# Lightning attention followed by a four-expert MoE: values and scores in one run, scores in two banks of the second product

## The chip, the cores and the metric

The kernel runs on one core of one Trainium2 chip. The metric is the device time of one execution in microseconds; the median of the runs counts. Everything is fp32.

## The reference

Two stages. The first is a linear attention with a decay per head, over 4 batches, 8 heads, 768 positions and 64 channels a head, in blocks of 64 positions with a running state:

```python
for b in range(nb):                                   # 12 blocks of 64
    intra = einsum('bhic,bhjc->bhij', qb, kb) * Dmask
    intra = einsum('bhij,bhjd->bhid', intra, vb)
    inter = einsum('bhid,bhde->bhie', qb * lam_pow, kv_state)
    out[:, :, sl] = intra + inter
    kv_state = lam_block * kv_state + einsum('bhsd,bhse->bhde', kb * rev_pow, vb)
```

Its output, laid out as x (3072 tokens by 512), goes through four experts that are all applied to every token:

```python
p = domain_probs / (domain_probs.sum(-1, keepdims=True) + 1e-09)
for e in range(4):                                    # w1[e] 512x1024, w2[e] 1024x512
    out += p[:, e:e+1] * (maximum(x @ w1[e], 0) @ w2[e])
```

## The kernel before

The tokens are cut into 24 chunks of 128 and three groups of eight chunks. A unit is one group through one expert; there are twelve units, 0 to 11, group by group. Both matrix products of a unit are computed in the manner of Strassen, as seven products of half-size blocks (M1 to M7). The products of the second layer of one unit (`second_product`, the matmuls at L1134, used in units 0 to 4) are interleaved with the products of the first layer of the next unit (`first_product`, L1075), which are themselves split into seven smaller products. All engines' orders are written out by hand: the program emits instructions in the order of the main loop, with a running slot count `now[0]`, and each engine executes its own in that order.

**Slots.** A unit has seven products, a product eight slots, so that slot s is (unit x 7 + product) x 8 + x. Slots take turns: a fourth of the second product (eight matmuls of 128x128 by 128x256 as the trace counts them), then a part of the first product (eight, in one slot of eight four). At the end of a slot come the vector and scalar work that was put off (`lately`, `background`, one item taken per slot), then the steps of the attention that are due in it, then loads and stores.

**The attention.** Chunks 0 to 7 (group 0) are computed in a prologue. Chunks 8 to 23 are computed in the main loop, in units 0 to 3, at slots that a formula gives: chunk n belongs to s = 24 + 12 x (n - 8).

- `load_more(n)` at s - 10 loads q and k (SP's queue, L174, or L114 for the chunks that come across); `load(n, "v")` at s - 6 loads v (L114).
- `turn(n)` at s brings q and k into the layout that scores need: eight PE transposes (L670) into PSUM banks s0 and s1, copied out by ScalarE, and q scaled from PSUM by VectorE. Chunks 16 to 23 come across: they are loaded from a DRAM buffer already in part turned, and two VectorE transposes of a whole tile (L652) take the place of those of PE.
- `scores(n)` at s + 5, or s + 6 for those that come across: 16 matmuls of q and k (L700) and 16 of v and k for the states (L707), all 64x64 (the trace records each twice), into banks s0 and s1. VectorE masks them into tile st and adds the states.
- `values(n)` at s + 10, or s + 12: 16 matmuls of the scaled q with the state (L754) and 16 of v with the masked scores (L772), again into s0 and s1. ScalarE copies the result out (L793).

Work on the chunk's tiles is put off by `soon` into `lately`, and taken at later slots, one item at a time; values forces what is still open. The decay of k is done on POOL. The state of a batch is one tile of two halves (for the two blocks of a chunk), of which POOL carries the first into the second.

**Banks.** PSUM has eight banks: s0, s1 for the attention, g1 and g3 for the first product, q01, q02, q11, q12 for the second. Of the second product's seven steps, in the order M1, M7, M4, M6, M2, M5, M3, the banks q02 and q12 are used by M7, M4 (steps 1, 2) and M2 (step 4); M1, M6, M5, M3 use q01 and q11. VectorE adds a bank's content to the results (L1152).

**Tiles.** q, k, v, the states, the masked scores and the sums of the first product all come out of one pool of 42 tiles of 128x512 (`small`), whose tags are shared: a load waits until the last reader of the tile that it replaces is done. All loads and stores of this stretch are issued by SP, in order (`send`, L114).

**The x blocks.** The output of the attention for group 1 goes to DRAM as seven blocks (`pair_sums`, `x_blocks`) and is fetched again by `x_fill`, which issues two loads (tile xs) and for some blocks differences on POOL, at slot 3 of each of seven successive products. `FILL` gives the product of the first. The first layer of group 1 starts at product 21, beside the last unit of group 0.

`forget`, called at the start of unit 4, takes all that is still open in `lately`.

Of the kernel before, what the change touches and what calls it, by code (L numbers as in the profile page):

```python
# [12 lines left out]
ALU = mybir.AluOpType  # L13
# [8 lines left out]
def kernel(  # L22
# [30 lines left out]
    nc = tc.nc  # L53
# [9 lines left out]
    CPG = 8  # L63
# [28 lines left out]
    def small(name):  # L92
        return pool.tile([P, W], FP32, name=name, tag="t")
# [22 lines left out]
    def tt(eng, o, a, b, op):  # L116
        eng.tensor_tensor(out=o, in0=a, in1=b, op=op)  # L117
        if eng is nc.gpsimd:
            busy[0] = max(busy[0], now[0]) + math.prod(o.shape[1:]) / (640 if spare else 480)
        else:  # L120
            vector(math.prod(o.shape[1:]), PSUM in (a.space, b.space))

    def vector(n, psum):
        filled[0] = max(filled[0], now[0] + psum / 2) + 0.09 + n * (0.31 if psum else 0.8 if spare else 0.49) / 512
# [29 lines left out]
    def after_of(n):  # L154
        c, b = where(n)
        return next((m for m in range(n + 1, NG * CPG) if where(m) == (c + 1, b)), None)
# [41 lines left out]
    def all_added(still=None):  # L198
        while adds and (still is None or adds[0][0] < still):
            adds.pop(0)[1]()  # L200
# [342 lines left out]
    def scale_q(qs, of):  # L543
        by = q_decay.unsqueeze(2).to_broadcast([P, NHP, 2, BL])
        tt(nc.vector, by_block(qs), by_block(of), by, ALU.mult)

    def passed(eng, o, s):
        tt(eng, o, s, q_decay[:, :, BL - 1:BL].to_broadcast([P, NHP, D]), ALU.mult)
# [68 lines left out]
    def soon(n, *work):  # L617

        if n < CPG:
            background[0:0] = work  # L620
            rest(len(work))
        else:
            lately.extend(work)
# [8 lines left out]

    carried = set()

    def begin_state(n):
        if where(n)[0] == 0 and n not in states:
            states[n] = small("kv")[:].rearrange("p (x h d) -> p x h d", x=2, d=D)
        if where(n)[0] and n in states and n not in carried:
            carried.add(n)
            passed(nc.gpsimd, states[n][:, 1], states[n][:, 0])  # L640

    def turn_across(n):

        qT, kT = nat.pop((n, "qx")), nat.pop((n, "kx"))
        qs = small("qs")

        def scaled():
            scale_q(qs, qT)
            turned[n] = qT, kT, qs

        def across(x):
            nc.vector.transpose(out=x[:], in_=x[:])  # L652
            vector(W, False)

        soon(n, *(lambda x=x: across(x) for x in (qT, kT)), scaled)

    def turn(n, tags):
        all_added()
        begin_state(n)
        if comes_across(n):  # L660
            turn_across(n)
            return
        if n < CPG:
            decayed(n)
        qn, kn = nat.pop((n, "q")), nat[n, "k"]
        qp = bank(tags[0], "qp")
        kp = bank(tags[1], "kp")
        for x, y in ((qp, qn), (kp, kn)):
            for ac in range(NHP):
                nc.tensor.transpose(  # L670
                    out=x[:, ac * C:(ac + 1) * C], in_=y[:, 2 * ac:2 * ac + 2].rearrange("p r d -> p (r d)"),
                    identity=ident[:],
                )
        if n >= CPG:
            decayed(n)
        del nat[n, "k"]
        qT, kT, qs = small("qT"), small("kT"), small("qs")
        nc.scalar.copy(out=qT[:], in_=qp[:])
        nc.scalar.copy(out=kT[:], in_=kp[:])
        scaled = lambda: scale_q(qs, qp)  # L680
        soon(n, scaled)
        turned[n] = qT, kT, qs, scaled

    def scores(n, tags):
        all_added()
        while n not in turned:
            take(lately, True)
        qT, kT = turned[n][0:2]
        while any(f in lately for f in turned[n][3:]):
            take(lately, True)  # L690
        begin_state(n)
        kd, vn = nat.pop((n, "kd")), nat[n, "v"]
        first, last = where(n)[0] == 0, where(n)[0] == NCH - 1

        sp = [bank(tags[r], "sp") for r in range(2)]
        blk = [slice(x * BL, (x + 1) * BL) for x in range(2)]
        for ac in range(NHP):
            for r in range(2):
                for x in range(2):
                    nc.tensor.matmul(  # L700
                        out=sp[r][half[x], ac * BL:(ac + 1) * BL], lhsT=hc(kT)[half[r], ac, blk[x]],
                        rhs=hc(qT)[half[r], ac, blk[x]], start=(ac == 0), stop=True, skip_group_check=True,
                    )
        for ac in range(NHP):
            for x in range(1 if last else 2):
                for r in range(2):
                    nc.tensor.matmul(  # L707
                        out=sp[x][half[r], 256 + ac * D:256 + (ac + 1) * D], lhsT=kd[half[x], 2 * ac + r],
                        rhs=vn[half[x], 4 * r + ac], start=False, stop=True, skip_group_check=True,
                    )  # L710
        st = small("st")
        added = [sp[x][:, 256:512].rearrange("p (h d) -> p h d", d=D) for x in range(2)]

        def mask(r):
            tt(
                nc.vector, st[:, r * 256:(r + 1) * 256], sp[r][:, 0:256], s_decay[:, r].rearrange("p h c -> p (h c)"),
                ALU.mult,
            )

        def middle():  # L720
            s = states[n][:, 1]
            if first:
                nc.scalar.copy(out=s, in_=added[0])
            else:
                tt(nc.vector, s, s, added[0], ALU.add)

        def end():
            s = states[after_of(n)] = small("kv")[:].rearrange("p (x h d) -> p x h d", x=2, d=D)
            passed(nc.vector, s[:, 0], states[n][:, 1])
            tt(nc.vector, s[:, 0], s[:, 0], added[1], ALU.add)  # L730

        work = [lambda: (mask(0), mask(1)), middle] + ([] if last else [end])
        soon(n, *work)
        masked[n] = st, work

    def values(n, tags):
# [15 lines left out]
        def inter(a, r, x, start):  # L752
            for y in range(2):
                nc.tensor.matmul(  # L754
                    out=op[r][half[y], cols(a, r) if x == r else apart(a)], lhsT=state[half[r], x, 2 * a + y],
                    rhs=by_block(qs)[half[r], 2 * a + y, x], start=start, stop=False, skip_group_check=True,
                )

# [55 lines left out]
            made.add(("blocks", g, x)),  # L814
        ))

    FILL = {1: 18, 2: 43}
    BEGIN = {1: (24, 12), 2: (24 + 12 * CPG, 12)}
    steps = []

    def attention(g):

        def put(slot, f):
            steps.append((slot, f))

        for i in range(CPG):
            n, s = g * CPG + i, BEGIN[g][0] + BEGIN[g][1] * i
            put(s - 10, lambda n=n: load_more(n))
            put(s - 6, lambda n=n: load(n, "v"))
            put(s, lambda n=n: turn(n, ("s0", "s1")))  # L830
            if comes_across(n):
                put(s - 2, lambda n=n: (decayed(n), nat.pop((n, "k"))))
            put(s + (6 if comes_across(n) else 5), lambda n=n: scores(n, ("s0", "s1")))
            put(s + (12 if comes_across(n) else 10), lambda n=n: values(n, ("s0", "s1")))
            if n == NG * CPG - 1:
                put(s + 17, turn_gates)
        steps.sort(key=lambda s: s[0])

    def forget():
        while lately:  # L840
            take(lately, True)
        assert not states


    rows = {
# [838 lines left out]
        "M2": ((), (), (("M3", 0, 0), ("M3", 0, 1)), (), (("M3", 1, 0), ("M3", 1, 1))),  # L1684
        "M4": ((("M5", 0),), (("M5", 1),), (("M2", 0),), (("M2", 1),)),
    }
    for g in range(1, NG):
        attention(g)
    PACE = 1.0, 1.0, 1.0
    FEED = (1, 5), (2, 5)  # L1690
    first_steps = first_result()
    for at, (g, e) in enumerate(units):
# [9 lines left out]
            chores.extend(prepare_w2_ops(1, True))  # L1702
            spare.append(True)
        if at == NEST - 1:
            forget()
            packed.append(True)
        blocks, banks = {}, {}
        for i in range(7):
# [40 lines left out]
            for x, part in enumerate(order):  # L1749
# [6 lines left out]
                if joins:  # L1756
                    joined()
                elif (ahead or x % 2 == 0 and x + i) and not (nests and i == 6 and x == 7):
                    if nested or nests:
                        rest()  # L1760
                    else:
                        took = False
                        for of in (lately, background, own_sums):
                            if of and (not took or fits() or of is background and len(of) > 1):
                                take(of)
                                took = True
# [22 lines left out]
                        x_fill(h, SEQ[at * 7 + i - FILL[h]])  # L1789
                pump(PACE[g])  # L1790
    pump(force=True)
    assert not (first_steps or ending or background or aside or chores or queue or late or results)


# [26 lines left out]
```

## Time and profile before

| what | value |
|---|---|
| median of three runs | 1157.88 us (1155.69 to 1158.87) |
| span of the profiled execution | 1157.0 us |
| PE (matmul) busy | 1143.7 us, 99% |
| PEld (weight load) busy | 991.6 us, 86% |
| VectorE (DVE) busy | 788.8 us, 68% |
| POOL busy | 771.7 us, 67% |
| ScalarE (ACT) busy | 369.8 us, 32% |
| HBM read, written | 194.83 MB, 77.10 MB |

The span is the time from the first to the last recorded instruction of one execution. Busy shares are averages; where an engine is on the path that sets the end is seen in its waits and in the chain that ended last. In that chain TensorE has 89% of the span, and the two products of the main loop that matter here have most of it: L1075 37% and L1134 20%. The costliest groups there (busy us in total, mean ns of one, then the idle time before them and what ended it):

```profile
L1075 PE MATMUL pg<-xs,ws_in 128*128 128x256 f32 x1960 | 472.9, 381 | 3.1 <-DVE m L117 2.9
L1134 PE MATMUL q<-w2t,m 128*128 128x256 f32 x1120 | 265.7, 380 | 0.5 <-DVE m L117 0.5
```

Matmuls are pipelined: each is on record for 380 ns, but the next starts before it ends. So the price of work on TensorE is read from the starts.

### The profile page before, as it was taken

The page shows a single profiled execution, that of the slowest core. Times are in us where ns is not written, and L with a number is a line of the kernel's source. Part 1 is how long each engine was busy: PE and PEld are TensorE (multiplying, and loading weights), DVE is VectorE, ACT ScalarE, POOL GpSimd, SP SyncE. Part 2 cuts the span into 40 slices and gives each one's busy share as a digit, 9 for nine tenths or more (in the row PEclk, how much of TensorE's full clock was granted, in tenths as well). Part 3 has the DMA queues.
Part 4 walks back from the last instruction along what each step waited for, and adds up shares of the span by engine and source line. Part 5 has one row for each costly group of instructions (what it writes and reads, how often), then busy time and mean ns, then how long its engine had stood idle before and what let it go on. Part 6 is the DMA issues. An engine that isn't in the chain of part 4 may idle for free.

```text
span 1157.0 us, 22155 instructions
## 1 busy us (share of the span) xinstructions
PE 1143.7 (99%) x8011; PEld 991.6 (86%) x8011; DVE 788.8 (68%) x1428; ACT 369.8 (32%) x745; POOL 771.7 (67%) x731
## 2 busy tenths in 40 slices
PE   8999999999999999999999999999999999999998
PEld 7888888888888888888888888888888888888887
DVE  3676775478477757835775567989775566676785
ACT  3422123222312321222244442343354442342332
POOL 2738318547742974873784998895995783873884
PEclk8999999999999999999999999999999999999999
DMA  8796668999899999896957667976777757657542
GB/s 189 181 276 190 185 178 243 291 295 282 264 319 311 267 304 303 264 352 180 293 189 243 185 203 252 344 225 202 220 244 247 214 175 196 196 160 215 167 191 74
DMA packets 309260, 269.22 MB, mean 233 GB/s; under 512 B 141536, under 2 KB 244128, under 8 KB 309152
## 3 DMA queue, kind: packets, MB, share of 16 engines
q1 hardware_dynamic: 290832, 262.53, 74.0%
q10 hardware_dynamic: 18320, 5.28, 2.3%
q8 instruction: 64, 1.05, 0.4%
q14 instruction: 44, 0.36, 0.1%
HBM read 194.83 MB, written 77.10 MB: 235 GB/s over the span
## 4 chain that ended last, share of the span: by engine, by line
PE 89%; DVE 5%; POOL 3%; issue 1%; DMA 1%; ACT 1%; ACTq 0%; SPq 0%; DVEq 0%; POOLq 0%
PE pg L1075 37%; PE pq L1433 20%; PE q L1134 20%; PE pM L1535 3%; DVE m L117 2%; PE pc L1535 2%; POOL acc L117 1%; PE sp L700 1%; DVE sums L117 1%; PE op L754 1%; PE op L772 1%; PE sp L707 1%; POOL ops L117 1%; DVE xs L117 1%; PE qp L670 1%
## 5 line engine op out<-in xcount | busy, mean ns | idle before, releaser
L1075 PE MATMUL pg<-xs,ws_in 128*128 128x256 f32 x1960 | 472.9, 381 | 3.1 <-DVE m L117 2.9
L1075 PEld LDWEIGHTS pg<-xs,ws_in 128*128 128x128 f32 x1960 | 368.7, 190 | 59.1 <-DVE m L117 8.9
L117 DVE TENSOR_TENSOR m<-pg,m 128x512 f32<-128x512 f32 x374 | 255.1, 686 | 102.0 <-PE pg L1075 90.4
L1134 PE MATMUL q<-w2t,m 128*128 128x256 f32 x1120 | 265.7, 380 | 0.5 <-DVE m L117 0.5
L1134 PEld LDWEIGHTS q<-w2t,m 128*128 128x128 f32 x1120 | 211.9, 190 | 30.1 <-DVE m L117 1.1
L117 POOL TENSOR_TENSOR m<-m,decay 128x512 f32<-128x512 f32 x91 | 115.6, 1284 | 89.4 <-ACT m L1092 62.8
L117 DVE TENSOR_TENSOR sums<-pq,sums 128x256 f32<-128x256 f32 x272 | 112.7, 420 | 85.7 <-PE pq L1433 77.7
L1433 PE MATMUL pq<-acc,w2t 128*128 128x256 f32 x688 | 169.2, 379 | 0.0
L1433 PEld LDWEIGHTS pq<-acc,w2t 128*128 128x128 f32 x688 | 130.5, 190 | 18.0
L1092 ACT ACTIVATE m<-m 128x512 f32<-128x512 f32 x99 | 62.4, 630 | 191.9 <-DVE m L117 189.9
L117 DVE TENSOR_TENSOR m<-m,m 128x512 f32<-128x512 f32 x112 | 100.4, 896 | 5.9 <-ACT m L1058 5.9
L1152 DVE SCALAR_TENSOR_TENSOR acc<-q,gate,acc 128x256 f32<-128x256 f32 x108 | 51.9, 480 | 75.3 <-PE q L1134 75.0
L1088 ACT COPY m<-pg 128x512 f32<-128x512 f32 x88 | 51.6, 586 | 123.8 <-PE pg L1075 122.4
L1052 ACT COPY pg<-m 128x512 f32<-128x512 f32 x77 | 45.4, 590 | 133.4 <-DVE m L117 126.2
L117 POOL TENSOR_TENSOR acc<-hT,hT 128x512 f32<-128x512 f32 x56 | 71.3, 1289 | 18.2 <-PE pq L1433 15.7
L117 POOL TENSOR_TENSOR acc<-hT,acc 128x512 f32<-128x512 f32 x56 | 71.4, 1275 | 8.5 <-PE pq L1433 4.7
L1433 PE MATMUL pq<-hT,w2t 128*128 128x256 f32 x288 | 70.0, 379 | 0.0
L117 POOL TENSOR_TENSOR w2o<-w2b 128x512 f32<-128x512 f32 x26 | 36.1, 1411 | 48.0 <-DMA w2b<-in_moe_w_dram 31.5
L1433 PEld LDWEIGHTS pq<-hT,w2t 128*128 128x128 f32 x288 | 54.5, 190 | 7.7
L1433 PE MATMUL pq<-m,w2t 128*128 128x256 f32 x228 | 55.5, 379 | 0.0
L117 POOL TENSOR_TENSOR xs<-xs 128x256 f32<-128x256 f32 x28 | 24.7, 884 | 43.3 <-DMA xs<-x_blocks 41.7
L907 ACT COPY hp<-m 128x512 f32<-128x512 f32 x84 | 48.4, 589 | 16.0 <-DVE hT L117 15.0
(145 smaller groups left out, 1443.2 us busy)
## 6 DMA issues: line engine op xcount, KB each, us to landing
w2t<-w_ops SPq DMA_DIRECT2D x129, 256.0 KB, 3.2
ws_in<-w_ops SPq DMA_DIRECT2D x40, 512.0 KB, 4.5
ws_in<-w_ops SPq DMA_DIRECT2D x60, 256.0 KB, 4.0
ws_in<-w_ops SPq DMA_DIRECT2D x40, 384.0 KB, 4.2
w2b<-in_moe_w_dram SPq DMA_DIRECT2D x56, 256.0 KB, 5.4
w_ops<-ops SPq DMA_DIRECT2D x28, 512.0 KB, 4.6
w2t<-w_sums SPq DMA_DIRECT2D x40, 256.0 KB, 4.6
w_sums<-w2o SPq DMA_DIRECT2D x16, 512.0 KB, 5.1
```

What stands on the lines that cost most here:

```text
L117: eng.tensor_tensor(out=o, in0=a, in1=b, op=op)
L670: nc.tensor.transpose(out=x[:, ac * C:(ac + 1) * C], in_=y[:, 2 * ac:2 * ac + 2].rearrange("p r d -> p (r d)"), identity=ident[:],)
L700: nc.tensor.matmul(out=sp[r][half[x], ac * BL:(ac + 1) * BL], lhsT=hc(kT)[half[r], ac, blk[x]], rhs=hc(qT)[half[r], ac, blk[x]], start=(ac ...
L907: nc.scalar.copy(out=there[x][:], in_=blk[at][:])
L1052: nc.scalar.copy(out=banks[tags[1]][:], in_=new["11"][:])
L1075: nc.tensor.matmul(out=p[:, j * 256:(j + 1) * 256], lhsT=ws[i][:, j * P:(j + 1) * P], rhs=xs[i], start=(fresh and j == 0), stop=True, skip ...
L1088: nc.scalar.copy(out=new[at][:], in_=p[:])
L1092: nc.scalar.activation(out=new[at][:], in_=new[at][:], func=AF.Relu)
L1134: nc.tensor.matmul(out=p[:, s * DH:(s + 1) * DH], lhsT=h[A_OF[m]][:, c * 256 + s * P:c * 256 + (s + 1) * P], rhs=fed2[g, e, m][uu][:, c], ...
L1152: nc.vector.scalar_tensor_tensor(out=o, in0=x, scalar=w, in1=o, op0=ALU.mult, op1=ALU.add)
L1433: nc.tensor.matmul(out=p[:, 0:256], lhsT=fed3[e, m, x // 2][:, x % 2, c * P:(c + 1) * P], rhs=b[B_OF[i]][:, c * 256:(c + 1) * 256], start= ...
L1535: nc.tensor.matmul(out=p[:, s * 256:(s + 1) * 256], lhsT=a[c][:, f:f + P], rhs=b[:, c, j * 256:(j + 1) * 256], start=(s == 0 and c == 0 an ...
```

## The change

In the main loop, chunks 8 to 23 are placed by a list of slots `AT` instead of a formula. At the slot of chunk n, the values of chunk n - 1 (in s0 and s1) and the scores of chunk n (now in q02 and q12) are emitted one right after the other. Around it:

- The turn stands 3 slots ahead of it, or 5 for chunks that come across; q and k are loaded 5 or 4 slots ahead of the turn, v 3 slots ahead of the scores. The k decay of chunks that come across is put 2 slots ahead of their turn.
- q is no longer scaled into a tile of its own out of PSUM: the copy of q is scaled in place after the scores, as the last item of the chunk's put-off work.
- The halves of a state are given out one by one out of a tile, and a new state takes a half.
- The x blocks of group 1 are fetched from product 20 on, not 18.
- `turn_gates` (the gates of the last group) stands 14 slots ahead of the last scores. `all_added` is told the current slot by `scores`; `forget` is gone; in unit 4, an open item of `lately` is taken ahead of `background`.

```diff
+    halves_of = {}
+
+    def state_half(x):
+        if not halves_of.get(x):
+            t = small("kv")
+            halves_of[x] = [t[:, y * 256:(y + 1) * 256].rearrange("p (h d) -> p h d", d=D) for y in range(2)]
+        return halves_of[x].pop(0)
+
     def begin_state(n):
         if where(n)[0] == 0 and n not in states:
-            states[n] = small("kv")[:].rearrange("p (x h d) -> p x h d", x=2, d=D)
+            states[n] = {}
         if where(n)[0] and n in states and n not in carried:
             carried.add(n)
-            passed(nc.gpsimd, states[n][:, 1], states[n][:, 0])
+            states[n][1] = state_half(1)
+            passed(nc.gpsimd, states[n][1], states[n][0])
 
     def turn_across(n):
         qT, kT = nat.pop((n, "qx")), nat.pop((n, "kx"))
-        qs = small("qs")
-
-        def scaled():
-            scale_q(qs, qT)
-            turned[n] = qT, kT, qs
 
         def across(x):
             nc.vector.transpose(out=x[:], in_=x[:])
             vector(W, False)
-
-        soon(n, *(lambda x=x: across(x) for x in (qT, kT)), scaled)
+            if x is kT:
+                turned[n] = qT, kT, qT
+
+        soon(n, *(lambda x=x: across(x) for x in (qT, kT)))
...
-        qT, kT, qs = small("qT"), small("kT"), small("qs")
+        qT, kT = small("qT"), small("kT")
         nc.scalar.copy(out=qT[:], in_=qp[:])
         nc.scalar.copy(out=kT[:], in_=kp[:])
+        if n >= CPG:
+            turned[n] = qT, kT, qT
+            return
+        qs = small("qs")
         scaled = lambda: scale_q(qs, qp)
...
     def scores(n, tags):
-        all_added()
+        all_added(now[0])
...
         def middle():
-            s = states[n][:, 1]
             if first:
-                nc.scalar.copy(out=s, in_=added[0])
+                states[n][1] = state_half(1)
+                nc.scalar.copy(out=states[n][1], in_=added[0])
             else:
+                s = states[n][1]
                 tt(nc.vector, s, s, added[0], ALU.add)
 
         def end():
-            s = states[after_of(n)] = small("kv")[:].rearrange("p (x h d) -> p x h d", x=2, d=D)
-            passed(nc.vector, s[:, 0], states[n][:, 1])
-            tt(nc.vector, s[:, 0], s[:, 0], added[1], ALU.add)
+            s = state_half(0)
+            states[after_of(n)] = {0: s}
+            passed(nc.vector, s, states[n][1])
+            tt(nc.vector, s, s, added[1], ALU.add)
 
         work = [lambda: (mask(0), mask(1)), middle] + ([] if last else [end])
+        if n >= CPG:
+            work.append(lambda: scale_q(qT, qT))
...
-    FILL = {1: 18, 2: 43}
-    BEGIN = {1: (24, 12), 2: (24 + 12 * CPG, 12)}
+    FILL = {1: 20, 2: 43}
+    AT = (26, 41, 49, 58, 82, 97, 103, 109, 115, 138, 153, 161, 170, 194, 209, 217)
     steps = []
 
-    def attention(g):
-
-        def put(slot, f):
-            steps.append((slot, f))
-
-        for i in range(CPG):
-            n, s = g * CPG + i, BEGIN[g][0] + BEGIN[g][1] * i
-            put(s - 10, lambda n=n: load_more(n))
-            put(s - 6, lambda n=n: load(n, "v"))
-            put(s, lambda n=n: turn(n, ("s0", "s1")))
+    def attention():
+
+        first, last = CPG, NG * CPG - 1
+        for n in range(first, last + 1):
+            s = AT[n - first]
+            turns_at = s - (5 if comes_across(n) else 3)
+
+            def both(n=n):
+                if n > first:
+                    values(n - 1, ("s0", "s1"))
+                scores(n, ("q02", "q12"))
+
+            steps.append((turns_at - (4 if comes_across(n) else 5), lambda n=n: load_more(n)))
+            steps.append((s - 3, lambda n=n: load(n, "v")))
+            steps.append((turns_at, lambda n=n: turn(n, ("s0", "s1"))))
             if comes_across(n):
-                put(s - 2, lambda n=n: (decayed(n), nat.pop((n, "k"))))
-            put(s + (6 if comes_across(n) else 5), lambda n=n: scores(n, ("s0", "s1")))
-            put(s + (12 if comes_across(n) else 10), lambda n=n: values(n, ("s0", "s1")))
-            if n == NG * CPG - 1:
-                put(s + 17, turn_gates)
+                steps.append((turns_at - 2, lambda n=n: (decayed(n), nat.pop((n, "k")))))
+            steps.append((s, both))
+        steps.append((AT[last - first] + 6, lambda: values(last, ("s0", "s1"))))
+        steps.append((AT[last - first] - 14, turn_gates))
         steps.sort(key=lambda s: s[0])
-
-    def forget():
-        while lately:
-            take(lately, True)
-        assert not states
...
         if at == NEST - 1:
-            forget()
             packed.append(True)
...
                     if nested or nests:
-                        rest()
+                        if lately:
+                            take(lately)
+                        else:
+                            rest()
```

More of the change, by code (lines that the diff above doesn't have):

```diff
@@ L754, in inter @@
                 nc.tensor.matmul(
-                    out=op[r][half[y], cols(a, r) if x == r else apart(a)], lhsT=state[half[r], x, 2 * a + y],
+                    out=op[r][half[y], cols(a, r) if x == r else apart(a)], lhsT=state[x][half[r], 2 * a + y],
                     rhs=by_block(qs)[half[r], 2 * a + y, x], start=start, stop=False, skip_group_check=True,
@@ L1686 @@
     }
-    for g in range(1, NG):
-        attention(g)
+    attention()
     PACE = 1.0, 1.0, 1.0
@@ L1791 @@
     pump(force=True)
-    assert not (first_steps or ending or background or aside or chores or queue or late or results)
+    assert not (states or lately or first_steps or ending or background or aside or chores or queue or late or results)
 _INS = ['q', 'k', 'v', 'lam', 'moe_domain_probs', 'moe_w1', 'moe_w2']
```

## The prediction

> **What bounds the kernel now.** I read the busy table and the slices first, then the windows over the stretch that the change touches (units 0 to 4, about 88 to 591 us), then PE's waits there. Of the page and the windows (span, then busy us of PE, PEld, DVE, ACT, POOL, granted clock, DMA share, GB/s):
>
> ```profile
> PE 1143.7 (99%) x8011; PEld 991.6 (86%) x8011; DVE 788.8 (68%) x1428; ACT 369.8 (32%) x745; POOL 771.7 (67%) x731
> ```
> ```profile
> 200.00:300.00 100.00, 99.10 (x988) 85.49 (x990) 66.58 (x116) 26.72 (x58) 62.90 (x68) 1.00 0.94 285
> 300.00:400.00 100.00, 99.89 (x916) 85.75 (x908) 71.09 (x126) 22.34 (x49) 58.81 (x61) 1.00 0.96 294
> ```
>
> TensorE is the bound, at full clock, with the DMA engines 94 to 96% busy beside it. Its waits in 88 to 515 us (total, times, longest, in us):
>
> ```profile
> PE qp L670 <- PE q L1134: 1.1, 2, 0.9
> PE pg L1075 <- DVE m L117: 0.2, 1, 0.2
> ```
>
> So the time can fall only by what TensorE spends between or inside its instructions, and it rises by every new wait.
>
> **The gain.** One scores run in the timeline of PE (start, duration, instructions):
>
> ```profile
> 204.76 1.89 PE L1075 MATMUL pg<-xs,ws_in 128*128 128x256 f32 x8
> 206.59 0.69 PE L700 MATMUL sp<-qT,kT 64*64 64x64 f32 x32
> 207.10 0.65 PE L707 MATMUL sp<-vn,kn 64*64 64x64 f32 x32
> 207.68 1.99 PE L1134 MATMUL q<-w2t,m 128*128 128x256 f32 x8
> ```
>
> Big matmuls start 0.2157 us apart, so eight take 1.73 us. The first group starts at 204.76 and the next big group at 207.68: 2.92 - 1.73 = 1.19 us for 64 small records; each of the 32 scores and values runs of chunks 8 to 23 costs this. A shorter run, in the prologue:
>
> ```profile
> 29.78 1.03 PE L1535 MATMUL pM<-xs,w1b 128*128 128x256 f32 x4
> 30.74 0.47 PE L754 MATMUL op<-qs,kv 64*64 64x64 f32 x16
> 31.02 0.66 PE L772 MATMUL op<-st,vn 64*64 64x64 f32 x32
> 31.61 1.13 PE L1535 MATMUL pM<-xs,w1b 128*128 128x256 f32 x4
> ```
>
> Here 48 records cost 1.83 - 4 x 0.2157 = 0.97 us. The 16 fewer save 0.22, 13.9 ns a record; 64 records are 0.89 us, and 1.19 - 0.89 = 0.30 us is paid per run, for going from 128x128 to 64x64 work and back. No merged run is in the trace; its saving is bounded by the visible gaps before and behind a run (0.10 + 0.13 = 0.23) and by 0.33, the longest that the weight loads stand idle there. I take 0.30. In the order of the two programs, values and scores stand as one unbroken run 15 times: 15 x 0.30 = **4.5 us** (3.4 to 5.0). The matmuls themselves are the same in number.
>
> The turns move too. Two of them waited, 1.1 us in all, for scores' or values' neighbours in the banks; their new slots lie elsewhere. I take **1.1 us** off (0 to 1.1).
>
> **Edits at nothing.** The state in two halves and the scaling out of SBUF in place of PSUM change DVE work: 0.68 us becomes 0.87 in 8 chunks, 1.5 us in 500, on an engine 67 to 71% busy; without that cover it would be 1.5 us. The scores use q02 and q12 when the second product has no use for them (its steps 3, 5, 6 and 0); by the order these banks must be free again two to six slots later, 3 us and more (a slot is eight matmuls or four). DVE needs two masks and two or three adds of 0.42 to 0.60 us, and is queued about 1 us (at most 3.4) behind TensorE: no wait taken, up to 1 us in 10 chunks if it comes late (a rival below). The half of the last states carried by POOL and the k decay have 5 to 6 us of lead, against 1.1 us of work and POOL up to 4.5 us behind: 0 (to 3).
>
> **What is fetched later.** This is the main cost. The loads of q, k and v and the x blocks of group 1 keep their number, but are issued much closer to their use. By the order, v is loaded 18 to 21 us before TensorE reads it now, and 6.1 us (nine chunks) or 6.4 to 7.0 (seven) after; natural q and k 16.5 to 18 now, 8.3 (six) or 10.4 (two) after; an x block about 35 now, 8.2 after. These are sums of slots (1.73 us, one in eight 0.86) and of the runs between. Against this, the view of tile vn (its loads and their landing) and of xs:
>
> ```profile
> L114 SPq DMA_DIRECT2D vn<-in_v_dram x16: 374/535/1012, 115.9 to 461.1; - x16
> ...
> DMA to landing us min/median/max: 3.0/4.9/9.5
> ```
> ```profile
> L114 SPq DMA_DIRECT2D xs<-x_blocks x14: 523/624/1400, 365.7 to 459.3; - x14
> ...
> DMA to landing us min/median/max: 3.3/4.1/7.9
> ```
>
> Landing takes 4.9 of the 6.1 us, so v bears 1.2 us of lateness of SP's queue. The queue is later than that. I matched the timelines of SP and PE by program order: a load's lateness is its issue less the start of the PE instruction that the order puts before it. Medians over stretches of 25 us from 100 on: -1.3, -3.6, 4.4, 5.8, 3.3, 4.2, 1.7, -0.4, 1.4, 4.7, 3.5, 2.4, 2.4, 3.7, 5.7. Loads landed behind that PE instruction by: v 1.35, 1.3, 8.3, 6.4, 13.0, 6.85, 11.65, 3.2, 5.5, 10.4, 8.3, 5.3, 6.6, 7.7, 6.4, 11.5; eight natural q/k up to 12.2; seven x blocks 6.6 to 14.9. What lies above the new leads sums to 26.2 (v) + 8.8 (q/k) + 11.9 (x) = 46.9 us: the upper bound, each lateness paid anew. The lower bound is 0: the queue's lateness has causes that the change also moves. SP's own waits in 100 to 500 us:
>
> ```profile
> SPq L174 <- PE sp L700: 7.9, 1, 7.9
> ...
> SPq L174 <- PE qp L670: 3.8, 1, 3.8
> ```
>
> Each is a q/k load that waits for a buffer, with everything behind it on SP; in the new order it is another load that takes that buffer.
>
> Between the bounds I reason so: when TensorE waits for a load, SP catches up by as much, so one crest of lateness is paid once, above the 1.2 us that v bears. The medians show three crests: 5.8, 4.7 (from -0.4, so anew) and 5.7 (from 2.4: between 1.0 above the crest before, if SP never recovers, and 4.5 anew; 2.75). That is 4.6 + 3.5 + 2.75 = **10.9 us**. Natural q/k (8.3 - 4.3 = 4.0 spare) and x (8.2 - 4.1) lie under the same crests and are not added.
>
> Chunk 16 is the first that comes across: by the order its kx transpose (0.70 us on DVE) stands 0.6 us ahead of its scores. With DVE about 1 us behind: **1.2 us** (0.7 to 2).
>
> **The sum**, against the profiled span: 1157.0 - 4.5 - 1.1 + 10.9 + 1.2 = 1163.5. The median of the runs, 1157.88, stands 0.9 above the profiled span: **1164.4 us**.
>
> **A rule against the row.** The Trainium skill, "DMA: Bandwidth & Descriptors", section "Anatomy of one DMA — SWDGE (gpsimd) path", fits one transfer by a fixed part of about 2 us plus bytes over 436 GB/s, which estimates 2.6 us for the 256 KB of v. The row says 4.9 (3.0 at least), with the DMA engines 95% busy, so the row decides; by the page v would bear 3.5 us, the crests would be 2.3 + 1.2 + 1.6 = 5.1, and the time 1158.6, an estimate near the second rival.
>
> **Rivals.**
> - *All arrives in time* (0.30): SP loses its two long buffer waits, the loads stand in it close to their use, and lateness stays below 1.2 us. Then only the gain: 1157.9 - 4.5 - 1.1 = 1152.3; faster. For it: the two waits of 7.9 and 3.8 us precede v loads that landed 8.3 to 13 behind. Against it: SP is late in most stretches, also without them, and the DMA engines are full.
> - *Break-even* (0.17): landing at its minimum of 3.0 us leaves v 3.1; the crests cost 2.7 + 1.6 + 1.8 = 6.1, and 1157.9 - 5.6 + 6.1 + 1.2 = 1159.6.
> - *Each lateness anew* (0.06): the x blocks fetched two products later land behind the first-product steps that read them, POOL's differences of them (0.73 to 0.88 us each) follow, and SP never recovers because the DMA engines are full: 1157.9 - 5.6 + 46.9 + 1.2 = 1200.4. It decides where SP is over 4 us late at the x loads (three of seven in the trace).
> - *The banks hold up the second product* (0.05): DVE frees q02 and q12 late, M7 and M2 wait 1 us in 10 chunks: 1152.3 + 10 = 1162.3. Against: TensorE waits for DVE only 0.2 us now.
>
> That the runs are not merged is excluded by the order.
>
> **How the numbers follow.** The forecast has the remaining 0.42. What a measurement can tell from no change is about 0.3%, 3.5 us. Faster holds the first rival, 0.30; same is break-even, 0.17; slower 0.42 + 0.06 + 0.05 = 0.53. The range runs from the first rival with the larger run gain (1157.9 - 5.0 - 1.1, rounded down to 1151.5) to 1178, the forecast with half of the bound of 46.9 in place of 10.9; both sides are needed, since the case of the other sign is not small. The forecast's own range is 1159 to 1178.
>
> **What would show it.** TensorE's waits in 88 to 515 us should name DMA of vn, of qn and kn, or of xs, or DVE and POOL behind them, some 5 to 25 us in all; a merged run of 128 records should cost 2.08 us. Chunks whose loads land under 6 us behind their PE mark should show no wait. If PE shows no wait for a load, the first rival holds; if the waits sit at the second product behind DVE, the bank rival; if they sit at the first product from about 370 us on, the x blocks.

## The result, and the profile after

The changed kernel takes 1163.28 us (median of five runs, 1161.22 to 1164.89), the kernel before 1157.88 us (also the median of five, 1155.69 to 1158.87); the ratio is 1.0047, with a 95% interval of 1.0029 to 1.0064. It is slower, by about 5.4 us. Ratios below are against runs of the kernel before on the same chip. The profiled execution has a span of 1161.7 us, 4.7 us more than before.

The busy table of the changed kernel, and two of its windows (span, busy us of PE, PEld, DVE, ACT, POOL, clock, DMA share, GB/s):

```profile
PE 1140.5 (98%) x8011; PEld 991.0 (85%) x8011; DVE 785.3 (68%) x1428; ACT 369.5 (32%) x745; POOL 773.5 (67%) x731
```
```profile
200.00:300.00 100.00, 98.83 (x944) 86.30 (x943) 66.99 (x121) 25.87 (x57) 58.09 (x62) 1.00 0.95 287
300.00:400.00 100.00, 96.45 (x883) 83.59 (x882) 69.67 (x124) 21.76 (x49) 61.52 (x63) 1.00 0.92 285
```

TensorE does the same number of matmuls in less busy time, yet between 300 and 400 us it is busy for 96.45 us of 100, where it was busy for 99.89. It waits. Its waits in 88 to 515 us, all of them (total, times, longest):

```profile
PE pg L1088 <- DVE m L117: 4.0, 3, 1.7
PE pg L1088 <- DMA xs<-x_blocks: 1.8, 1, 1.8
PE sp L717 <- POOL w2o L117: 1.5, 1, 1.5
PE pg L1088 <- POOL xs L117: 0.4, 1, 0.4
PE sp L710 <- DVE kx L656: 0.4, 1, 0.4
PE sp L717 <- DMA w1b<-in_moe_w_dram: 0.2, 1, 0.2
```

Before, there were 1.3 us of waits. L1088 is the first product (L1075 before), L717 the second half of scores, which reads v. The two waits at L717 end when a load of v lands: two loads of v landed at 346.68 and 478.52, and L717 began at 346.76 and 478.65. That POOL and another load are named there can be put down to work of theirs that ended at about the same time. A merged run, in the timeline of PE:

```profile
159.27 1.03 PE L1088 MATMUL pg<-xs,ops 128*128 128x256 f32 x4
160.22 0.69 PE L768 MATMUL op<-qT,kv 64*64 64x64 f32 x32
160.74 0.65 PE L786 MATMUL op<-st,vn 64*64 64x64 f32 x32
161.21 0.65 PE L710 MATMUL sp<-qT,kT 64*64 64x64 f32 x32
161.67 0.65 PE L717 MATMUL sp<-vn,kn 64*64 64x64 f32 x32
162.25 1.99 PE L1147 MATMUL q<-w2t,m 128*128 128x256 f32 x8
```

From 159.27 to 162.25 are 2.98 us; the four big matmuls in it take 0.86, so the run costs 2.12 us, where two runs apart cost 2 x 1.185. An account of all gaps between the starts of TensorE's instructions, from the start of the first to the start of the 35th product of the main loop (491.4 us before, 496.7 after), closes. Counted from starts, a wait is some 0.2 us longer than the idle time that the list above shows:

| term | us |
|---|---|
| 15 merged runs, 0.25 each | -3.8 |
| turns (two waits gone) | -1.3 |
| v late, inside the scores runs | +2.35 |
| kx late for chunk 16 | +0.6 |
| x blocks and POOL's differences of them late (445.8, 447.3) | +2.6 |
| VectorE late for the first product (276.6, 383.5, 488.5 and small ones) | +4.85 |
| sum | +5.3 |

Outside of this stretch the two executions differ by 0.6 us the other way.

The largest term is one that no load explains. VectorE before the wait at 276.60, in the timeline (the brackets give idle time and what ended it):

```profile
268.55 0.48 DVE L1165 SCALAR_TENSOR_TENSOR acc<-q,gate,acc 128x256 f32<-128x256 f32 x1 [2.64 <-PE q L1147]
268.95 0.75 DVE L117 TENSOR_TENSOR st<-sp,decay 128x256 f32<-128x256 f32 x2
269.62 0.68 DVE L117 TENSOR_TENSOR m<-m,m 128x512 f32<-128x512 f32 x1
270.21 0.48 DVE L117 TENSOR_TENSOR xc<-xc,op 128x128 f32<-128x128 f32 x2
...
273.33 0.93 DVE L117 TENSOR_TENSOR kv<-kv,decay 128x256 f32<-128x256 f32 x1
274.30 0.42 DVE L117 TENSOR_TENSOR kv<-kv,sp 128x256 f32<-128x256 f32 x1
274.64 1.31 DVE L117 TENSOR_TENSOR m<-m,m 128x512 f32<-128x512 f32 x1
275.87 0.68 DVE L117 TENSOR_TENSOR m<-pg,m 128x512 f32<-128x512 f32 x1
276.47 1.15 DVE L117 TENSOR_TENSOR qT<-qT,decay 128x512 f32<-128x512 f32 x1
```

and TensorE there:

```profile
273.76 1.67 PE L1147 MATMUL q<-w2t,m 128*128 128x256 f32 x7
276.60 1.99 PE L1088 MATMUL pg<-xs,ws_in 128*128 128x256 f32 x8 [1.17 <-DVE m L117]
```

From 268.55 until TensorE goes on, VectorE is never idle: behind the merged run come its masks (st), the adds of the values of the chunk before (xc), the state's decay and sums (kv) and the scaling of q (qT), between the sums of the products (m, acc). At 275.87 it reads the bank that TensorE wants, ends at 276.55, and TensorE goes on at 276.60. Over the whole kernel VectorE has less to do than before (785.3 us against 788.8); it is its order and crowding that changed.

Crowding is not all of it. The sum of m at 274.64 takes 1.31 us, where the same sum takes 0.68 at 269.62. Ahead of the waits at 383.48 and 488.50, VectorE is likewise busy without a break (from 375.81 and from 481.30), and there too such sums are slow:

```profile
381.62 1.21 DVE L117 TENSOR_TENSOR m<-m,m 128x512 f32<-128x512 f32 x1
484.90 1.35 DVE L117 TENSOR_TENSOR m<-m,m 128x512 f32<-128x512 f32 x1
```

POOL is at work beside each of the three. What these sums take over 0.68 us adds up to 1.8 us, against 4.0 us of waits for VectorE. No run separates this from the crowding; but slow sums alone do not make the difference, since they are as frequent in the kernel before (between 88 and 515 us, 30 of the 97 sums m<-m,m take over 0.9 us there, and 28 in the changed kernel).

### The profile page after: what moved, and what is told of

The parts are those of the page before. It is cut to its first block, busy times and chain, and to the rows that moved or that the text cites. A ratio compares the mean times of both kernels' runs of the same rounds, so it can differ in the third digit from the quotient of the medians.

```text
span 1161.7 us, 22129 instructions
## 1 busy us (share of the span) xinstructions
PE 1140.5 (98%) x8011; PEld 991.0 (85%) x8011; DVE 785.3 (68%) x1428; ACT 369.5 (32%) x745; POOL 773.5 (67%) x731
## 4 chain that ended last, share of the span: by engine, by line
PE 86%; DVE 6%; DMA 4%; issue 1%; POOL 1%; SPq 1%; ACT 0%; ACTq 0%; DVEq 0%; POOLq 0%
PE pg L1088 36%; PE pq L1446 22%; PE q L1147 17%; DVE m L117 3%; PE pM L1548 2%; PE pc L1548 2%; PE op L768 1%; DVE sums L117 1%; DMA w1b<-in_moe_w_dram 1%; PE sp L710 1%; PE sp L717 1%; PE op L786 1%; SPq L114 1%; DVE xs L117 1%; PE qp L676 1%
## 5 line engine op out<-in xcount | busy, mean ns | idle before, releaser
L1088 PE MATMUL pg<-xs,ws_in 128*128 128x256 f32 x1960 | 472.0, 380 | 8.6 <-DVE m L117 6.1
L1088 PEld LDWEIGHTS pg<-xs,ws_in 128*128 128x128 f32 x1960 | 369.7, 190 | 65.9 <-DVE m L117 14.5
L117 POOL TENSOR_TENSOR kn<-kn,decay 128x512 f32<-128x512 f32 x16 | 17.7, 1108 | 105.5 <-PE kp L676 39.8
```

The costliest lines, as they stand in the source:

```text
L1088: nc.tensor.matmul(out=p[:, j * 256:(j + 1) * 256], lhsT=ws[i][:, j * P:(j + 1) * P], rhs=xs[i], start=(fresh and j == 0), stop=True, skip ...
```

## The experiments

Each is an edit of the changed kernel unless it says otherwise. The waits are those of the profiled execution, in 88 to 515 us.

**The merged run undone.**

```diff
             def both(n=n):
-                if n > first:
-                    values(n - 1, ("s0", "s1"))
                 scores(n, ("q02", "q12"))
+            if n > first:
+                steps.append((s + 1, lambda n=n: values(n - 1, ("s0", "s1"))))
```

> The changed kernel with one edit: the values of chunk n-1 are emitted one slot after the scores of chunk n, not right before them (same banks, same loads, same slots else). Theory: the 15 merged runs save what the trace of the changed kernel shows, 1.19 + 1.19 - 2.12 = 0.26 us each, so apart is 3.9 us slower, about 1167, with 32 runs of 1.19 us; unless VectorE's adds of the values, which now come a slot later, thin out its burst, then 1165. Rival: running them together is worth nothing, or the burst that it makes costs more than it saves: 1163 or less.

Measured: 1168.3 us, ratio 1.0104 (1.0086 to 1.0121), some 6.6 us above the changed kernel by the ratios. The runs stand apart at 1.185 us each again, so 3.8 us come from there. The rest is within the spread: the waits add up to about the same (7.9 us against 8.3), only at other places (2.5 us for VectorE against 4.0, but 1.9 for v, 1.5 for kx, 1.5 for x). So the gain is there, and the loss is not made by putting the two together.

**Loads earlier, one kind at a time.**

```diff
-            steps.append((s - 3, lambda n=n: load(n, "v")))
+            steps.append((s - 6, lambda n=n: load(n, "v")))
```

> The changed kernel with v loaded 6 slots ahead of the scores, not 3. Theory: v is late only where the trace shows L717 waiting until vn landed (1.49 us at 346.8, 0.22 at 478.6), so 1.7 us less: 1161.6, and the other waits stay. Rival, as predicted: v's lateness is most of the loss, 10.9 us: 1153 to 1157.

Measured: 1164.8 us, 1.0073 (1.0053 to 1.0092). Both theories missed. No wait for v is left, but those for x and POOL's work on it grew from 2.2 to 3.3 us, those for VectorE from 4.0 to 5.0, and behind the two waits at 443 and 445 the clock fell to 0.50, from 446.0 to 449.4 (see the end).

```diff
-    FILL = {1: 20, 2: 43}
+    FILL = {1: 18, 2: 43}
```

> The changed kernel with FILL back at 18 (x blocks of group 1 fetched two products earlier, as before the change). Theory: the waits of TensorE for tile xs and POOL's differences of it (2.0 and 0.6 us at 445.8 and 447.3) go: 1160.7. Rival: the tiles that the earlier x blocks hold make loads of q, k and v wait for buffers, and the time stays or rises (1163 to 1166).

Measured: 1162.8 us, 1.0047 (1.0034 to 1.0059): no change. The waits for x are gone as foreseen, and in their place are waits for v (1.0 us at 493.5), for natural q and k (0.8) and others. In both profiles the lateness is handed to other loads, and neither edit alone brings a gain.

**Both together.** The two edits above in one kernel.

> The changed kernel with v 6 slots ahead of the scores and FILL at 18: both edits of the two runs before, which each moved waits to another load. Theory: the lateness belongs to SP's queue and is paid by the next load with a short lead, here the natural q and k and those that wait for tiles of the common pool: 1161 to 1164. Rival: v and x blocks are each late by themselves, and with both early the 4.3 us of waits for loads go: 1159.

Measured: 1160.2 us (twelve runs), 1.0020 (1.0009 to 1.0032), 3.1 us better than the changed kernel by the ratios (whose intervals overlap by a little). The theory fell; the rival was nearer, and its waits for loads did go. TensorE's waits in this run:

```profile
PE pg L1088 <- DVE m L117: 5.3, 6, 1.9
PE sp L717 <- issue: 1.5, 1, 1.5
PE sp L710 <- DVE kx L656: 0.4, 1, 0.4
```

No load is seen waited for any more, and 5.3 us for VectorE are left. ("issue" is a wait for nothing that the profile shows; it lies inside a run, at 449.16, and the v of that run had landed at 442.45. Its cause stays open.) That the leads are then long enough was tried with v and q/k 8 slots ahead:

> As both_early, with v 8 slots ahead of the scores and q and k 8 ahead of the turn (all loads close to the leads of the kernel before). Theory: the trace of both_early shows no wait for a load any more, so nothing is left to win by leads: 1160. Rival: the runs of both_early hold waits that the profiled one did not have, 1157 to 1158. Rival: the 42 tiles of the common pool are taken longer and SP waits for them: over 1162.

Measured: 1159.9 us, 1.0018 (1.0005 to 1.0031), the same.

**The late loads alone, in the kernel before.** Runs apart, old slots and banks:

```diff
-            put(s - 10, lambda n=n: load_more(n))
-            put(s - 6, lambda n=n: load(n, "v"))
+            put(s - (4 if comes_across(n) else 5), lambda n=n: load_more(n))
+            put(s + (3 if comes_across(n) else 2), lambda n=n: load(n, "v"))
...
-    FILL = {1: 18, 2: 43}
+    FILL = {1: 20, 2: 43}
```

> The kernel before with nothing changed but its loads: q and k 5 slots (4 for chunks that come across) ahead of the turn, v 3 slots ahead of the scores, FILL at 20, as in the changed kernel; runs stay apart, in their old slots and banks, VectorE's work stays spread. Theory: this alone brings the waits for loads, 4 to 6 us: 1162 to 1164, and next to no wait of TensorE for VectorE. Rival, as predicted: the late loads cost 10.9 us or more: 1169. Rival: late loads cost nothing without the crowding that the new slots make: 1158.

Measured: 1169.0 us, 1.0101 (1.0079 to 1.0124), 11.7 us slower: the size that the rival took over from the prediction, not that of the theory. Here v is read sooner after its load than in the changed kernel, where the values run of 1.2 us stands between as well. Its profiled execution (span 1164.2) is a mild one and shows one long wait of TensorE, and a second price behind it (the waits, then a window of 5 us with its clock of 0.50):

```profile
PE sp L707 <- DMA vn<-in_v_dram: 5.7, 3, 5.1
PE pg L1075 <- DVE m L117: 0.6, 2, 0.4
```
```profile
190.00:195.00 5.00, 5.00 (x33) 3.98 (x27) 0.71 (x2) 0.00 (x0) 2.07 (x3) 0.50 0.46 121
```

After 5.07 us of waiting the big matmuls start 0.43 us apart until 195.3, not 0.2157. So late loads cost time without any crowding, and with chunks evenly apart VectorE is waited for only 0.6 us.

**Another queue for the same loads.**

```diff
-                    send(out=to[:, h], in_=of[:, h])
+                    send(out=to[:, h], in_=of[:, h], by=nc.scalar if n >= CPG else None, count=True)
...
                 in_=x_blocks[g - 1, :, :, BLOCK_AT[m], a * C:(a + 1) * C],
+                by=None if g == LAST else nc.scalar, count=True,
```

(`count=True` keeps the program's own count of what has been sent, so that the rest of its order stays.)

> The changed kernel with the loads of v (chunks 8 to 23) and of the x blocks of group 1 issued by ScalarE's queue instead of SP's, at the same slots. Theory: it is SP's queue that is late (6.7 us at the x block at 435.6, 2.8 at v at 338), not the transfers (3.4 to 5.9 us there), so with ScalarE's queue v and x land in time, and 4 of the 8.4 us of new waits go: 1159; those for VectorE stay. Rival: the DMA engines are full and the transfers get longer instead: 1163. Rival: ScalarE waits for the buffers, and its copies of TensorE's banks come late: over 1165.

Measured: 1167.1 us, 1.0078 (1.0060 to 1.0096). v is waited for less (0.6 us), but the transfers take longer: 6.1 us in the median for v (4.8 in the changed kernel) and 6.0 for x (4.6, at most 10.4), and TensorE waits for POOL's differences of the x blocks:

```profile
PE pg L1089 <- POOL xs L117: 5.1, 4, 2.5
```

Three of these four waits (2.6 us) end when an x block has landed and POOL has done its first difference. The fourth and longest, at 448.7, does not: its block had landed by 442.81, but POOL, in order, waited for a load of k first (9.9 us, to 445.3), which SP still issued. Behind that wait the clock was 0.50 until 452.3. So the first rival has the mechanism (the transfers got longer, with the DMA engines 92 to 95% busy between 200 and 500 us), the time is nearer to that of the second, and another queue for a part of the loads does not bring them earlier.

**VectorE's burst.** Without the scaling of q, whose last place in the put-off work is kept:

```diff
-            work.append(lambda: scale_q(qT, qT))
+            work.append(lambda: vector(W, False))
```

> The changed kernel without the scaling of q for chunks 8 to 23 (the output is then without the decay of q between blocks in these chunks): 16 instructions of 0.92 to 1.04 us less on VectorE, at the end of each chunk's burst of put-off work. Theory: TensorE's waits for VectorE (1.3 us at 276.6, 1.8 at 383.5, 1.4 at 488.5) come from this burst; two or three of them go, 3 to 4.5 us less: 1159 to 1160. Rival: VectorE is late for another reason (loads that it waits for): 1163.

Measured: 1162.8 us, 1.0046 (1.0031 to 1.0062). The waits for VectorE fell from 4.0 to 2.1 us as expected (at 383 and 488, not at 276, where the scaling stands behind the read). The time did not follow: the x blocks came 4.5 us late in all, and behind that the clock was 0.50 from 444.0 to 450.8. With the scaling on POOL (`nc.gpsimd` in place of `nc.vector`):

> The changed kernel with the scaling of q (chunks 8 to 23) on POOL instead of VectorE. In the run without the scaling TensorE's waits for VectorE fell to about 2 us but its waits for x blocks grew, and the time stayed. Theory: the waits for VectorE fall here too, and as POOL has its 16 x 1.1 us more, its differences of the x blocks and of k come later: 1161 to 1164, no gain that can be told. Rival: VectorE's burst is the main loss and POOL has room (58 to 70% busy): 1159.

Measured: 1170.8 us, 1.0111 (1.0091 to 1.0131), far worse than either said; the lines that tell why, among TensorE's waits:

```profile
PE op L768 <- POOL qT L117: 3.4, 3, 1.9
PE op L768 <- POOL qx L117: 3.3, 2, 3.0
PE pg L1088 <- DVE m L117: 1.9, 2, 1.2
```

The next chunk's values read the scaled q, and POOL, in order behind its other sums, was not done. VectorE's wait is halved, to 1.9 us, and 6.7 us of waits for POOL come in; the clock also falls to 0.50 twice (480.2 to 483.6 and 497.3 to 500.7).

On top of both_early, the scaling put back ahead of the scores, into a tile of its own and for natural chunks out of PSUM:

```diff
+        qs = small("qs")
+        def scaled():
+            scale_q(qs, qT)
+            turned[n] = qT, kT, qs
...
-            if x is kT:
-                turned[n] = qT, kT, qT
-        soon(n, *(lambda x=x: across(x) for x in (qT, kT)))
+        soon(n, *(lambda x=x: across(x) for x in (qT, kT)), scaled)
...
-        if n >= CPG:
-            turned[n] = qT, kT, qT
-            return
         qs = small("qs")
         scaled = lambda: scale_q(qs, qp)
...
-        if n >= CPG:
-            work.append(lambda: scale_q(qT, qT))
```

> As both_early (v 6 slots ahead, FILL 18; 1160.2), and the scaling of q put back to where the kernel before had it: into a tile of its own, ahead of the scores, for natural chunks out of PSUM (0.68 us, against 1.04 now). Theory: the burst of put-off work behind a merged run is what makes VectorE late (5.3 us of waits of TensorE for it in both_early); it loses its last member, and the waits at 381 and 486 fall as they did without the scaling, to about 3 us in all: 1158. Rival: VectorE's work is only moved, and it is as late at another place: 1160. Rival: the tile more in the common pool makes loads wait: over 1162.

Measured: 1160.5 us, 1.0016 (1.0003 to 1.0029): not to be told from both_early, though its profiled execution has a span of 1155.8 and 4.4 us of waits for VectorE.

On top of both_early, the chunks four to each unit:

```diff
-    AT = (26, 41, 49, 58, 82, 97, 103, 109, 115, 138, 153, 161, 170, 194, 209, 217)
+    AT = (26, 41, 49, 58, 82, 97, 105, 114, 138, 153, 161, 170, 194, 209, 217, 226)
...
-    FILL = {1: 18, 2: 43}
+    FILL = {1: 19, 2: 43}
```

> As both_early, but the slots of the chunks are the same four in each unit (26, 41, 49, 58 and so on by 56), where the changed kernel has 4, 5, 4 and 3 in a unit and three gaps of 6 slots; FILL 19, since group 1 ends later. Theory: the wait of 1.3 us at 276 stands among the chunks that are 6 slots apart and goes; those at 381 and 486, among chunks 8 or 9 apart, stay: 1158.5 to 1159. Rival: spacing is not it, all waits for VectorE stay: 1160, or more by the x blocks.

Measured: 1158.9 us, 1.0006 (0.9997 to 1.0015): the kernel before is reached. The wait of 1.3 us among the chunks 6 slots apart shrank to 0.2 (counted from starts), as the theory had it; the others stay (at 378, 481 and 486), and VectorE is waited for 4.8 us in all, against 5.3 in both_early. The intervals of the two runs overlap, so this step alone is not shown to gain. The last run has all three: loads early, four chunks a unit, scaling first.

> even_slots (1158.9) with the scaling of q ahead of the scores, as in scale_first: the loads early, the chunks four to a unit, the last member of VectorE's burst moved. Theory: the waits of TensorE for VectorE at 374 to 378 and 481 to 486 (4.8 us in even_slots) fall to about 3, and the version lies 1 to 2 us below even_slots and about 1 below the kernel before: 1157. Rival: scaling first won nothing that its runs show (1160.5 against 1160.2 in both_early) and wins nothing here: 1159.

Measured: 1156.5 us (1154.49 to 1157.25), 0.9986 (0.9975 to 0.9997): faster than the kernel before by 0.14%, with the interval just short of one. In its profile (span 1154.7) TensorE waits for one thing only:

```profile
PE pg L1087 <- DVE m L117: 3.6, 3, 1.8
```

## Why the prediction was right, and where it was not

The direction and the time were right (1164.4 us forecast, 1163.28 measured, the forecast's own case), and so was its main mechanism: loads issued closer to their use make TensorE wait. That the time came out within 1.1 us is luck, though: late loads were put 5.9 us too high, and VectorE, which makes 4.85 us of waits, was put at nothing.

- **The merged runs**: 4.5 us forecast, 3.8 measured. The step of 0.30 us a run came from the difference between a run of 48 records in the prologue and one of 64 in the main loop; the merged run shows 0.25, near the 0.23 of the visible gaps. It was mis-sized, within its bounds, and the price per record under it does not hold: in the main loop of the kernel before, four runs have 48 records (at 366.50, for one), and they cost 1.17 us, not 0.97.
- **The turns**: 1.1 forecast, 1.3 measured.
- **Late loads** were forecast as the main cost, 10.9 us. In the trace v and x cost 5.0, and taking the late leads away wins 3.1 us (both_early, by the ratios): the mechanism is shown, the size was two to three and a half times too large. Two things failed in the estimate. It carried over the lateness of SP's queue from the old order (crests of 4.7 to 5.8 us), but in the new order SP was early, or at most 1.3 us late, at ten of the 16 v loads, and v paid only 2.35. And "x lie under the same crests and are not added" did not hold: x waited on its own (2.6 us), after 6.7 us of lateness of SP's queue at 435.6. The picture of one lateness that the next load pays fits v_early and x_early, in which it passed to other loads; the sum over three crests did not come. In the kernel before, the same late loads cost 11.7 us, with less work between load and use: so 10.9 was about the price of late loads in the old slots, though part of the 11.7 is the half clock behind a wait, which the prediction did not have.
- **kx of chunk 16**: 1.2 forecast, 0.6 measured, at the place foreseen.
- **"Edits at nothing"** is the step that failed. It gave VectorE's work a cover of 30% idle time, an average, and a lateness of about 1 us, taken from the old slots, which were 12 apart. The new ones are 6 to 9 apart in clusters, since q02 and q12 are free for scores only beside the second product's steps 3, 5, 6 and 0. There its cover is gone, and TensorE pays 4.85 us. The scaling out of SBUF also costs more than the 0.87 taken from the trace: 1.04 us for natural chunks (0.92 for those that come across). The slow ones coincide with work on POOL: between 272.9 and 279 us, where POOL is never idle, VectorE's sum of m takes 1.31 and 1.21 us, against 0.68 alone at 269.62. The Trainium skill, "SBUF — State Buffer", section "SBUF: two separate sides", says that a VectorE instruction with two operands in SBUF and a GpSimd instruction that reads SBUF lock one port pair against each other, so that the one that starts second waits for the other to end. The trace agrees: in the kernel before, the scaling of natural chunks reads one operand from PSUM and takes 0.68 us in all eight, in six of them with POOL at work beside it; that of the chunks that come across reads both from SBUF and takes 0.67 to 0.68 us with POOL idle and 0.71 to 1.53 with POOL at work.
- **The rivals.** The bank rival named the right engine and the wrong place: TensorE waits for VectorE at the first product, never at the second, so in the changed kernel the banks q02 and q12 are free in time. "All arrives in time" and "each lateness anew" did not happen in the changed kernel. both_early is about the former, and took 1160.2 us, not 1152.3; of the 7.9 us between, the merged runs' smaller gain is 0.7, and the waits for VectorE in its trace (of an execution that took 1162.4) are 5.3.
- **The rule against the row.** The row was right to decide: in the changed kernel v landed after 4.8 us in the median and 3.3 at least, not 2.6. The Trainium skill, "DMA: Bandwidth & Descriptors", section "Anatomy of one DMA — SWDGE (gpsimd) path", gives its fit for transfers issued by GpSimd, and v is issued by SP.
- **The range.** Its upper end, the forecast with half of 46.9 in place of 10.9, comes to 1177, not 1178. Nothing hangs on it.

What stays open: the waits for VectorE stand at the same three places in most of these kernels, but the loss was never taken back by removing them alone: in no_scale they halved, and late x blocks and the clock took the gain. So their full price is inferred from the account of the trace and from even_slots and even_scale, whose intervals overlap or touch the neighbouring ones. How much of it is crowding and how much is POOL's work beside VectorE was not separated either. And single profiled executions can be milder than the median run: in before_late 1164.2 us of span against 1169.0.

## What to carry to other kernels

Merging small runs on the engine that bounds a kernel gained here what the gaps in the trace said (0.25 us a run); what it cost was decided by where the merged work could stand. Check the new slots on every engine that serves them, as they are bunched, and not by that engine's average: here VectorE, 70% busy, kept TensorE waiting at three places where put-off work stood 6 to 9 slots apart. And shorten loads' leads, if at all, together with a look at the lateness of the queue that issues them: here moving one kind of load ahead again only passed the wait on, and moving both took it away.

## What was not expected of the hardware

A wait of TensorE can cost more than itself. Behind 5.07 us of waiting the clock was 0.50 until 195.4 (before_late); it also fell to 0.50 behind two waits of 2.0 and 1.5 us close together (no_scale, with some four matmuls between), behind a single wait of 2.45 us (act_queue, 448.8 to 452.3) and behind one of 1.73 us inside a run of 64x64 matmuls (pool_scale, 480.2 to 483.6), but not behind 1.85 and 0.44 us (the changed kernel, 1.00). The Trainium skill, "TensorE: Matmul & The Clock Gate", section "Why this matters for your kernels", warns of idle gaps above some 3 us. The wait of 5.07 us agrees with it; the others show that shorter waits can have the same effect, and that their length alone does not decide it.
